# Query weights folded in small array tiles and earlier, output weights split later, key sums copied by ScalarE: a gated mix of linear attention and a dense layer

## The chip, the core and the metric

The kernel runs on one core of a Trainium2 chip. The core's engines run side by side and wait for one another by semaphores: TensorE (PE in the profile; its weight loads are PEld), VectorE (DVE), ScalarE (ACT), GpSimd (POOL) and SyncE (SP), which here only issues DMAs. Matmuls write to PSUM, eight banks of 128 partitions by 512 numbers; everything else lies in SBUF. The metric is the time of one execution on the device, in microseconds (us), as a median over several runs. The profile shows one execution, taken by the hardware profiler.

## What is computed

Two branches over the same 2048 rows of 512 numbers, mixed by a gate of each row, all in float32:

```python
g = _sigmoid((x * gate_w).sum(-1, keepdims=True))
qkv = (x @ wqkv).reshape(B, S, 3, H, Dh)            # H = 32 heads, Dh = 16
pq = jnp.einsum("bhsd,hdf->bhsf", q, w_phi)         # the same for pk from k
phi_q = jnp.concatenate([_softmax(pq), _softmax(-pq)], axis=-1)
kv = jnp.einsum("bhsf,bhsd->bhfd", phi_k, v)
z  = jnp.einsum("bhsf->bhf", phi_k)
o = jnp.einsum("bhqf,bhfd->bhqd", phi_q, kv) / (jnp.einsum("bhqf,bhf->bhq", phi_q, z)[..., None] + 1e-6)
a = o.reshape(B, S, D) @ wo
h = x @ w1 + b1                                     # F = 1792
b = jnp.square(jnp.maximum(h, 0)) @ w2 + b2
return g * a + (1 - g) * b
```

The query projection is followed by a small matrix for each head, so the two can be multiplied once, ahead of all rows: wq times w_phi. The kernel calls this the fold.

## The kernel before

Every large product is made of three matmuls, because each operand is held as a high and a low part (`mm3`, L74 to L78; `split`, L61, makes the two parts: a copy that rounds, then a subtraction). A full matmul has a 128 by 128 stationary operand and 512 columns.

The dense layer gives the order of everything. `work_list` (L843) goes twice over the four blocks of 512 rows, with seven of the fourteen hidden tiles each time. Item t of it makes one hidden tile (`up`, 12 matmuls into a bank named u), two items ahead of its use, and then adds an earlier one to the four output banks (`down`, 12 matmuls into d). All other work is hung between these by hand: `at(step, f, ...)` (L785) files a function under a half step, and the main loop (L870) runs steps 2t, 2t + 0.5, 2t + 1 and 2t + 1.5 ahead of the up product, in its middle, behind it, and in the middle of the down product. So item 25 covers steps 50 to 51.5. Each engine runs its own queue in the order that a scheduler made from this program order and from when it expected things to be ready. `tc.high_priority(offset=AHEAD)` puts an instruction 150 places ahead in that order; `tc.issue_after(i)` keeps an instruction behind i on i's engine.

In the first half of the run (items 0 to 27) the keys are projected, turned into features and multiplied with the values; the key weights were folded at step 5.5 by `tiles_fold` (L175), which works in 32 by 32 tiles of the array, one bank for each of the four row strips. The last key-value product (`kv`, L710) stands at step 53.5. In the second half (items 28 to 55) a pair of row tiles of queries starts every 6 steps from 56.5 on: projection (`do_q`), features (`do_phi`, whose transposed pieces go to phiT by twelve DMAs on SP and four ScalarE copies), the numerator (`do_n`, L380) and the output product with wo (`finish`).

What the change touches:

- `do_wT` (L456) at step 49 loads the query weights and w_phi into five buffers of the tag row, of which there are six. Two tiles of gate rows and the room for the key sums (`kv_room`, step 51) use the same tag.
- `do_fold` (L459) at steps 53, 54, 55 and 56 makes one quarter of the folded query weights each: four full-array float32 matmuls of 128 columns into a bank (`fold`, L148), then the split by ScalarE and VectorE straight from the bank. [...]
- `bank` (L53) hands out the small PSUM banks in turn. At steps 51 to 55 there are three of them: a, e and f. Bank b holds the key sums until `kv_done`.
- `wo_load` and `wo_split` (L235, L241): the output weights, in four tiles, at steps 50.5 to 53.5 and 52 to 55. They use the tag in of the pool `stage`, with four buffers, like the dense weights (`ffn_load`, the last at step 56) and the x tiles (`do_x`, step 61 for the next block). `behind()` (L69) keeps a split behind the newest hidden tile's on ScalarE and VectorE.
- `kv_done` (L747) at step 55 copies the key sums out of their bank by four VectorE copies of 17 partitions and sends the row of sums to DRAM and back to all partitions (z), where the query features need it.
- `gated` (L443) takes the four output banks, times the gate, out at the end of each block.

Of the kernel before, what the change touches and what calls it, by code (L numbers as in the profile page):

```python
# [7 lines left out]
F32 = mybir.dt.float32  # L8
F32R = mybir.dt.float32r
# [6 lines left out]
P = 128  # L16
S, D, H, DH, F = 2048, 512, 32, 16, 1792
NK = D // P
# [16 lines left out]
def tile_gated_mix(ctx: ExitStack, tc: tile.TileContext, xT, xn, wqT, wkT, wphi, wv, wo, w1, b1, w2, b2, gw, out):  # L35
# [112 lines left out]
    def fold(loaded, nm, k):  # L148
        wph, *t = loaded
        ps = bank(f"fold{nm}{k}")  # L150
        for g in range(NK):
            nc.tensor.matmul(ps[:, g * P:(g + 1) * P], t[g][:, k * P:(k + 1) * P], wph[:, g * P:(g + 1) * P],
                             start=True, stop=True)
        hi = wpool.tile([P, 512], F32R, tag=f"wah{k}", name=f"w{nm}h{k}")
        lo = wpool.tile([P, 512], F32R, tag=f"wal{k}", name=f"w{nm}l{k}")
        with tc.high_priority(offset=AHEAD):
            split(ps, hi, lo, nc.scalar, nc.vector)
        return hi, lo

# [14 lines left out]

    def tiles_fold(loaded):  # L175
        wph, *t = loaded
        pss = [bank(f"fold{r}") for r in range(4)]

        def mm(g, r, c):
            rows, cols = slice(32 * r, 32 * r + 32), slice(32 * c, 32 * c + 32)  # L180
            return nc.tensor.matmul(pss[r][cols, g * P:(g + 1) * P],
                                    wph[rows, g * P + 32 * r:g * P + 32 * r + 32],
                                    t[g][rows, :].rearrange("p (k c q) -> p k c q", c=4, q=32)[:, :, c, :],
                                    start=True, stop=True, skip_group_check=True)

        last = None
        for x in [(g, r, c) for g in range(NK) for c in range(4) for r in range(4)]:
            with tc.issue_after(last.ins) if last else nullcontext():
                last = mm(*x)
        for half in range(2):  # L190
            tb = work.tile([P, 2, 4, NK, 32], F32, tag="tb", name="turned", bufs=2)
            for r in range(2):
                with tc.high_priority(offset=AHEAD):
                    st["turned"] = nc.vector.transpose(tb[:, r].rearrange("p g k q -> p (g k q)"), pss[2 * half + r])
            for k in range(NK):
                dst = st["raw"][k].rearrange("p (h z g r f) -> p h z g r f", h=2, z=2, g=2, r=4)
                for h in range(2):
                    nc.scalar.activation(dst[:, h, 0, :, 2 * half:2 * half + 2],
                                         tb[:, :, 2 * h:2 * h + 2, k].rearrange("p r g q -> p g r q"), AF.Copy)

# [258 lines left out]
    def do_fold(nm, k):  # L459
        with tc.issue_after(st["up"].ins):  # L460
            st["wa", nm, k] = fold(st["wT"], nm, k)
        if k == NK - 1:
            st["wa"] = [st["wa", nm, i] for i in range(NK)]
            if nm == "k":
                banks.pop()

# [190 lines left out]
    def pair_steps(p, s):  # L657
# [52 lines left out]
        def kv():  # L710
# [3 lines left out]
            with tc.issue_after(later.ins):  # L714
                kv_chunk(False, p == LASTP, st["kv"], v["phi", n], v["v", n])
# [31 lines left out]
    def kv_done():  # L747
        kvps, kvs = st["kv"], st["kvs"]
        for j in range(4):
            s = slice(32 * j, 32 * j + VW)  # L750
            nc.vector.tensor_copy(kvs[s, :], kvps[s, :])
# [60 lines left out]
    at(49, do_wT, wqT)  # L812
    for k in range(NK):
        at(53 + k, do_fold, "q", k)
    for k in range(NK):
        at(base + 8.5 + k, wo_load, k)
        at(base + 10 + k, wo_split, k)
# [52 lines left out]
    for t, (sw, b, i) in enumerate(work_list):  # L870
# [17 lines left out]
        for c in range(NC):  # L888
# [12 lines left out]
            for j, s in enumerate(halves if end else (ALL,)):  # L901
                gated(ends[j] if end else dps[c], n, o, s)
# [49 lines left out]
```

## Time and profile before

| what | value |
|---|---|
| median of 3 runs | 507.05 us (506.77 to 507.06) |
| the profiled execution | 507.18 us, span 505.4 us |
| granted TensorE clock in it | 0.999 |
| PE busy | 500.7 us of the span |
| VectorE busy | 407.0 us |
| ScalarE busy | 256.6 us |

The profile's page has busy times by engine, a strip of the span in 40 slices, the DMA queues, the chain of work that ended last, and the groups of instructions that cost most. The trace behind it can be asked for instructions in order of time (start, duration, engine, line, operation, output<-input, shape, count), for groups by line and shape (busy time, mean ns of one, idle time before them), for waits, and for DMAs with their time to landing. In a row like `u<-xh,w1h` u is what is written and the rest what is read. Matmuls are pipelined, so a matmul's duration is longer than the distance to the next start, and the distances are what counts on PE.

### The profile page before, as it was taken

How to read it: one execution, taken by the hardware profiler on the slowest of the kernel's cores; microseconds unless marked ns; L12 is line 12 of the kernel's file. 1: busy time of each engine (PE TensorE's matmuls, PEld its weight loads, DVE VectorE, ACT ScalarE, POOL GpSimd, SP SyncE). 2: the span in 40 equal slices, each digit the busy share in tenths (PEclk: the TensorE clock that was granted, in tenths of full speed). 3: DMA queues.
4: the chain of work that ended last, by engine and by line, in shares of the span. 5: the costliest groups of instructions: out<-in, count | busy, mean ns of one | idle time of the engine just before them, and what ended most of it. 6: DMA issues, size and time to landing. Idle time of an engine off the chain costs nothing.

```text
span 505.4 us, 9354 instructions
## 1 busy us (share of the span) xinstructions
PE 500.7 (99%) x3520; PEld 406.1 (80%) x3520; DVE 407.0 (81%) x680; ACT 256.6 (51%) x458; POOL 87.3 (17%) x102
## 2 busy tenths in 40 slices
PE   9999999999999999999999999999999999999997
PEld 5878888788888888888888878788787878788776
DVE  5569957988695979796998989897979796897724
ACT  4887655565253474454674744454455353333540
POOL 1000151204410035000013040212222221112200
PEclk9999999999999999999999999999999999999999
DMA  8858587756854578771265311325112231041112
GB/s 261 291 196 273 198 305 225 237 190 234 285 184 165 183 223 294 265 228 65 83 211 209 98 49 48 99 64 150 49 31 90 71 86 43 8 131 57 38 27 83
DMA packets 45829, 76.13 MB, mean 151 GB/s; under 512 B 6868, under 2 KB 23000, under 8 KB 45784
## 3 DMA queue, kind: packets, MB, share of 16 engines
q1 hardware_dynamic: 36072, 41.78, 26.6%
q10 hardware_dynamic: 6768, 23.79, 13.7%
q0 software_dynamic: 2944, 9.96, 5.5%
q8 instruction: 28, 0.46, 0.4%
q14 instruction: 17, 0.14, 0.1%
HBM read 57.68 MB, written 11.54 MB: 137 GB/s over the span
## 4 chain that ended last, share of the span: by engine, by line
PE 98%; DMA 1%; DVE 0%; issue 0%
PE d L76 10%; PE d L77 10%; PE d L78 10%; PE u L76 10%; PE u L77 9%; PE u L78 9%; PE pX L653 3%; PE q L77 3%; PE att L77 3%; PE att L78 3%; PE att L76 3%; PE q L78 3%; PE q L76 3%; PE pX L655 3%; PE pX L654 3%; PE pY L655 2%
## 5 line engine op out<-in xcount | busy, mean ns | idle before, releaser
L421 ACT ACTIVATE r<-u,b1c 128x512 f32<-128x512 f32 x56 | 38.5, 687 | 122.9 <-PE u L78 121.2
L76 PE MATMUL d<-w2h,hh 128*128 128x512 f32 x222 | 86.9, 391 | 0.0
L77 PE MATMUL d<-w2l,hh 128*128 128x512 f32 x222 | 86.4, 389 | 0.0
L78 PE MATMUL d<-w2h,hl 128*128 128x512 f32 x222 | 86.4, 389 | 0.0
L76 PE MATMUL u<-xh,w1h 128*128 128x512 f32 x212 | 83.6, 394 | 0.0
L77 PE MATMUL u<-xl,w1h 128*128 128x512 f32 x212 | 82.6, 390 | 0.0
L78 PE MATMUL u<-xh,w1l 128*128 128x512 f32 x212 | 82.5, 389 | 0.0
L333 POOL TENSOR_TENSOR ez<-e,z 128x512 f32<-128x512 f32 x32 | 42.9, 1360 | 165.0 <-ACT e L309 165.0
L66 DVE TENSOR_TENSOR hl<-r,hh 128x512 fp32r<-128x512 f32 x56 | 37.8, 676 | 24.3 <-ACT hh L63 24.1
L76 PEld LDWEIGHTS d<-w2h,hh 128*128 128x128 f32 x222 | 41.7, 188 | 9.2 <-issue 0.6
L76 PEld LDWEIGHTS u<-xh,w1h 128*128 128x128 f32 x212 | 39.8, 188 | 11.1 <-issue 2.9
L78 PEld LDWEIGHTS d<-w2h,hl 128*128 128x128 f32 x222 | 41.7, 188 | 8.7
L77 PEld LDWEIGHTS d<-w2l,hh 128*128 128x128 f32 x222 | 41.7, 188 | 8.5
L78 PEld LDWEIGHTS u<-xh,w1l 128*128 128x128 f32 x212 | 39.8, 188 | 8.6 <-DVE w1l L66 0.2
L77 PEld LDWEIGHTS u<-xl,w1h 128*128 128x128 f32 x212 | 39.8, 188 | 7.9
L309 ACT ACTIVATE e<-e 128x1024 f32<-128x1024 f32 x27 | 28.6, 1059 | 26.5 <-DVE e L307 26.1
L291 DVE TENSOR_REDUCE sm<-e 128x64 f32<-128x1024 f32 x27 | 32.8, 1215 | 10.8 <-ACT e L309 10.8
L63 ACT ACTIVATE hh<-r 128x512 fp32r<-128x512 f32 x56 | 35.2, 628 | 1.1
L423 ACT ACTIVATE r<-r 128x512 f32<-128x512 f32 x56 | 34.9, 624 | 0.7
L692 ACT ACTIVATE tmp<-pX 128x512 f32<-128x512 f32 x24 | 14.4, 598 | 30.6 <-PE pX L655 27.0
L374 ACT ACTIVATE phiT<-tb 32x256 f32<-32x256 f32 x64 | 26.4, 412 | 5.8 <-DVE tb L359 4.9
L343 DVE TENSOR_REDUCE dz<-ez 128x64 f32<-128x1024 f32 x16 | 19.4, 1212 | 11.7 <-POOL ez L333 11.7
(182 smaller groups left out, 984.2 us busy)
## 6 DMA issues: line engine op xcount, KB each, us to landing
sloto<-wkeep ACTq DMA_DIRECT2D x30, 512.0 KB, 4.6
in<-in_xT SPq DMA_DIRECT2D x42, 256.0 KB, 4.4
slotez<-wkeep ACTq DMA_DIRECT2D x15, 512.0 KB, 5.0
phiT<-tb SPq DMA_DIRECT2D x192, 32.0 KB, 1.8
in<-in_w SPq DMA_DIRECT2D x23, 256.0 KB, 3.3
part<-row POOLq DMA_DIRECT2D x16, 256.0 KB, 5.5
row<-part SPq DMA_DIRECT2D x16, 256.0 KB, 3.0
out<-row SPq DMA_DIRECT2D x15, 256.0 KB, 2.2
```

The lines of the kernel that those rows point to most:

```text
L63: i = nc.scalar.activation(hi, src, AF.Copy)
L66: st["lo"] = elo.tensor_tensor(lo, src, hi.bitcast(F32), ALU.subtract)
L76: nc.tensor.matmul(o, ah[:, sa], bh[:, sb], start=first, stop=False)
L77: nc.tensor.matmul(o, ah[:, sa], bl[:, sb], start=False, stop=False)
L78: return nc.tensor.matmul(o, al[:, sa], bh[:, sb], start=False, stop=last)
L291: nc.vector.tensor_reduce(sm, e3, AX.X, ALU.add)
L309: nc.scalar.activation(ef, ef, AF.Exp)
L333: nc.gpsimd.tensor_tensor(ez[:, hs, :], e3[:, hs, :], zbc[half], ALU.mult)
L374: nc.scalar.activation(dst, src, AF.Copy)
L421: st["relu"] = nc.scalar.activation(r, ps, AF.Relu, bias=b1c[:, fc:fc + 1])
L423: nc.scalar.activation(r, r, AF.Square)
L655: nc.tensor.matmul(ps, l, wh, start=False, stop=j == 1, skip_group_check=True)
```

## The change

The four full-array folds go. In their place `query_fold` makes the folded query weights in two halves, at steps 51.5 and 54: 32 matmuls each of a 32 by 32 stationary tile and 128 columns, over two row strips of the array into two banks; two VectorE transposes of 32 by 32 squares out of these banks (`turned`, at high priority); and four splits of 256 columns from the turned tile. `tiles_fold` for the keys is written with the same helpers and does what it did. The output weights are loaded at steps 58 to 61 and split at 59.5 to 62.5. The key sums leave their bank by ScalarE copies at high priority. `kv` now notes its last matmul, so that the second half fold stands behind it on PE, and the gated sums of the last block of the first pass are kept behind the newest hidden tile's subtraction on VectorE.

```diff
--- before.py
+++ after.py
@@ -145,18 +145,6 @@
             nc.sync.dma_start(t[g + 1], wT[:, g, :])
         return t
 
-    def fold(loaded, nm, k):
-        wph, *t = loaded
-        ps = bank(f"fold{nm}{k}")
-        for g in range(NK):
-            nc.tensor.matmul(ps[:, g * P:(g + 1) * P], t[g][:, k * P:(k + 1) * P], wph[:, g * P:(g + 1) * P],
-                             start=True, stop=True)
-        hi = wpool.tile([P, 512], F32R, tag=f"wah{k}", name=f"w{nm}h{k}")
-        lo = wpool.tile([P, 512], F32R, tag=f"wal{k}", name=f"w{nm}l{k}")
-        with tc.high_priority(offset=AHEAD):
-            split(ps, hi, lo, nc.scalar, nc.vector)
-        return hi, lo
-
     def both(t):
         return t[:, :512], t[:, 512:]
 
@@ -172,31 +160,47 @@
             st["raw"][k] = r
             st["wv"] = nc.sync.dma_start(two(r)[:, :, 256:], two(wv[k * P:(k + 1) * P, :]))
 
+    def fold_block(loaded, out, g, r, c):
+        wph, *t = loaded
+        rows, cols = slice(32 * r, 32 * r + 32), slice(32 * c, 32 * c + 32)
+        return nc.tensor.matmul(out[cols, g * P:(g + 1) * P], wph[rows, g * P + 32 * r:g * P + 32 * r + 32],
+                                t[g][rows, :].rearrange("p (k c q) -> p k c q", c=4, q=32)[:, :, c, :],
+                                start=True, stop=True, skip_group_check=True)
+
+    def turned(pss, half):
+        tb = work.tile([P, 2, 4, NK, 32], F32, tag="tb", name="turned", bufs=2)
+        for r in range(2):
+            with tc.high_priority(offset=AHEAD):
+                st["turned"] = nc.vector.transpose(tb[:, r].rearrange("p g k q -> p (g k q)"), pss[2 * half + r])
+        return tb
+
     def tiles_fold(loaded):
-        wph, *t = loaded
-        pss = [bank(f"fold{r}") for r in range(4)]
-
-        def mm(g, r, c):
-            rows, cols = slice(32 * r, 32 * r + 32), slice(32 * c, 32 * c + 32)
-            return nc.tensor.matmul(pss[r][cols, g * P:(g + 1) * P],
-                                    wph[rows, g * P + 32 * r:g * P + 32 * r + 32],
-                                    t[g][rows, :].rearrange("p (k c q) -> p k c q", c=4, q=32)[:, :, c, :],
-                                    start=True, stop=True, skip_group_check=True)
-
+        pss = {r: bank(f"fold{r}") for r in range(4)}
         last = None
-        for x in [(g, r, c) for g in range(NK) for c in range(4) for r in range(4)]:
+        for g, c, r in [(g, c, r) for g in range(NK) for c in range(4) for r in range(4)]:
             with tc.issue_after(last.ins) if last else nullcontext():
-                last = mm(*x)
+                last = fold_block(loaded, pss[r], g, r, c)
         for half in range(2):
-            tb = work.tile([P, 2, 4, NK, 32], F32, tag="tb", name="turned", bufs=2)
-            for r in range(2):
-                with tc.high_priority(offset=AHEAD):
-                    st["turned"] = nc.vector.transpose(tb[:, r].rearrange("p g k q -> p (g k q)"), pss[2 * half + r])
+            tb = turned(pss, half)
             for k in range(NK):
                 dst = st["raw"][k].rearrange("p (h z g r f) -> p h z g r f", h=2, z=2, g=2, r=4)
                 for h in range(2):
                     nc.scalar.activation(dst[:, h, 0, :, 2 * half:2 * half + 2],
                                          tb[:, :, 2 * h:2 * h + 2, k].rearrange("p r g q -> p g r q"), AF.Copy)
+
+    def query_fold(half):
+        pss = {r: bank(f"fold{r}") for r in (2 * half, 2 * half + 1)}
+        for g, c, r in [(g, c, r) for g in range(NK) for c in range(4) for r in pss]:
+            with tc.issue_after(st["up"].ins):
+                st["up"] = fold_block(st["wT"], pss[r], g, r, c)
+        tb = turned(pss, half)
+        part_ = lambda t: t.rearrange("p (g r f) -> p g r f", g=NK, f=32)[:, :, 2 * half:2 * half + 2, :]
+        for k in range(NK):
+            if not half:
+                st.setdefault("wa", []).append(tuple(
+                    wpool.tile([P, 512], F32R, tag=f"wa{hl}{k}", name=f"wq{hl}{k}") for hl in "hl"))
+            hi, lo = st["wa"][k]
+            split(tb[:, :, :, k].rearrange("p r g q -> p g r q"), part_(hi), part_(lo), nc.scalar, nc.vector)
 
     def operand(i, j, src, slot=None, ehi=None, elo=None):
         if i in HELD:
@@ -455,14 +459,6 @@
 
     def do_wT(wT):
         st["wT"] = load_fold(wT)
-
-    def do_fold(nm, k):
-        with tc.issue_after(st["up"].ins):
-            st["wa", nm, k] = fold(st["wT"], nm, k)
-        if k == NK - 1:
-            st["wa"] = [st["wa", nm, i] for i in range(NK)]
-            if nm == "k":
-                banks.pop()
 
     def do_joint(j, piece):
         if (j, piece) == (0, 0):
@@ -712,7 +708,7 @@
                 st["kv"] = ps_b.tile([P, 2 * P], F32, tag="s", name="kvps")
             later = kv_chunk(p == 0, False, st["kv"], v["phi", m], v["v", m])
             with tc.issue_after(later.ins):
-                kv_chunk(False, p == LASTP, st["kv"], v["phi", n], v["v", n])
+                st["up"] = kv_chunk(False, p == LASTP, st["kv"], v["phi", n], v["v", n])
 
         at(s - 2 - (p > 0), sums_load, p)
         if p == 0:
@@ -748,7 +744,8 @@
         kvps, kvs = st["kv"], st["kvs"]
         for j in range(4):
             s = slice(32 * j, 32 * j + VW)
-            nc.vector.tensor_copy(kvs[s, :], kvps[s, :])
+            with tc.high_priority(offset=AHEAD):
+                nc.scalar.activation(kvs[s, :], kvps[s, :], AF.Copy)
         nc.sync.dma_start(zrow.rearrange("(j x) -> j x", j=4), kvs[DH::32, :])
         for half in range(2):
             z = hold.tile([P, H * VW], F32, tag="vz", name=f"z{half}")[:, :D]
@@ -810,11 +807,11 @@
         pair_steps(p, 14 + 4.5 * p)
     base = (NB - 1) * SL
     at(49, do_wT, wqT)
+    at(51.5, query_fold, 0)
+    at(54, query_fold, 1)
     for k in range(NK):
-        at(53 + k, do_fold, "q", k)
-    for k in range(NK):
-        at(base + 8.5 + k, wo_load, k)
-        at(base + 10 + k, wo_split, k)
+        at(base + 16 + k, wo_load, k)
+        at(base + 17.5 + k, wo_split, k)
     for i in range(NFH):
         for nm, slot in (("w1", base + 2 * i - 1), ("w2", base + 2 * i + 2)):
             at(slot, ffn_load, nm, NFH + i)
@@ -899,7 +896,8 @@
             dst = part[n] if sw == 0 else out[n * P:(n + 1) * P, :]
             end = t == last and c == NC - 1
             for j, s in enumerate(halves if end else (ALL,)):
-                gated(ends[j] if end else dps[c], n, o, s)
+                with tc.issue_after(st["dve"].ins) if (sw, b) == (0, NB - 1) else nullcontext():
+                    gated(ends[j] if end else dps[c], n, o, s)
                 if sw == 0 or done:
                     st["stored"] = (nc.gpsimd if sw == 0 else nc.scalar if j else nc.sync).dma_start(dst[:, s], o[:, s])
```

## The prediction

> **What bounds the kernel now.** I read the page first: busy times, then the chain that ended last.
>
> ```profile
> span 505.4 us, 9354 instructions
> PE 500.7 (99%) x3520; PEld 406.1 (80%) x3520; DVE 407.0 (81%) x680; ACT 256.6 (51%) x458; POOL 87.3 (17%) x102
> PE 98%; DMA 1%; DVE 0%; issue 0%
> ```
>
> A busy PE alone proves little, because matmul ends are modelled; the chain of waits is the stronger evidence: 98% of it is PE, one matmul after another. So I asked for PE's waits, all of them, and for PE's rows in a quiet stretch.
>
> ```profile
> PE pX L653 <- DMA sloto<-wkeep: 0.2, 1, 0.2
> ...
> 236.55 0.39 PE L76 MATMUL u<-xh,w1h 128*128 128x512 f32 x1
> 239.27 0.39 PE L76 MATMUL d<-w2h,hh 128*128 128x512 f32 x1
> ```
>
> Once it has its first operand, PE waits a single time in the run, for 0.2 us, and not near the change. Between the two rows lie twelve full matmuls: 2.72 us, so 0.227 us from one start to the next. The reader is to see a kernel that is the sum of what PE streams. The change can gain only what PE no longer streams, and loses whatever PE newly waits for. Less work for ScalarE or VectorE is worth nothing in itself. The calibrated span is 505.4 us, that execution took 507.18 us and the median of the runs is 507.05; the costs below are that execution's, and I subtract them from the median, 0.13 us lower.
>
> **The change part by part. The folds on PE.** The chain lists each old query fold, four in all; here are the first and the last.
>
> ```profile
> 244.87 0.89 PE foldq L152 x8
> 257.19 0.89 PE foldq L152 x8
> ...
> 244.48 0.39 PE L78 MATMUL u<-xh,w1l 128*128 128x512 f32 x1
> 245.83 0.40 PE L77 MATMUL d<-w2l,hh 128*128 128x512 f32 x1
> ```
>
> PE's own rows agree (the last two): the full matmul before a fold starts at 244.48, the second one after it at 245.83, which is 1.35 less two pitches, 0.90 us. Four folds are 4 x 0.89 = 3.56 us, and all of it goes.
>
> What comes instead is known from this kernel twice over. The key weights are already folded with 32 by 32 tiles, all four row strips at once (L181), and the attention numerator (L385) runs on eight array tiles, as many as a half of the new fold uses (two row strips by four column strips).
>
> ```profile
> 26.15 0.39 PE L78 MATMUL d<-w2h,hl 128*128 128x512 f32 x1
> 26.46 1.90 PE L181 MATMUL fold<-row 32*32 32x128 f32 x128
> 28.30 0.50 PE L76 MATMUL d<-w2h,hh 128*128 128x512 f32 x1
> 28.63 0.40 PE L77 MATMUL d<-w2l,hh 128*128 128x512 f32 x1
> ...
> 297.15 0.39 PE L78 MATMUL u<-xh,w1l 128*128 128x512 f32 x1
> 297.47 1.09 PE L385 MATMUL num<-phiT,kvb 64*32 64x256 f32 x32
> 298.83 0.40 PE L77 MATMUL u<-xl,w1h 128*128 128x512 f32 x1
> ```
>
> The key fold holds PE from 26.15 to 28.63, 2.48 less two pitches: 2.03 us, of which 1.84 is the fold and 0.19 the two switches of shape (0.31 and 0.33 where 0.23 is the pitch). Half of it, with 64 of the 128 records, would be 0.92 + 0.19 = 1.11 if the overlap stays as it is: that is the lower bound. The numerator streams 32 records of 256 columns on eight tiles, as many columns as 64 records of 128: 1.68 less 0.45, or 1.23 us with its switches. The upper bound is that half as many tiles give half the overlap, so that a half takes as long as the whole, 2.03. I take the numerator's 1.23, because it has the same eight tiles; two halves are 2.46. **PE's own sum: 3.56 - 2.46 = 1.10 us gained**, with ends 3.56 - 2.22 = 1.34 and 3.56 - 4.06 = -0.50.
>
> [...]
>
> **The loads.** The first half runs at step 51.5, where PE now stands at 240.63; the old first fold came at 244.87. The last of its five loads waits for a row buffer.
>
> ```profile
> 236.05 0.35 SPq L145 DMA_DIRECT2D row<-in_wqT  x1
> DMA to landing us min/median/max: 3.1/3.1/3.1
> 240.63 0.39 PE L76 MATMUL d<-w2h,hh 128*128 128x512 f32 x1
> ```
>
> It lands at 239.15, 1.5 us early, and only the last quarter of the half reads it: no wait, though the cover shrinks by four us.
>
> **ScalarE and VectorE.** The groups by shape give the prices.
>
> ```profile
> L66 DVE TENSOR_TENSOR wql<-foldq,wqh 128x512 fp32r<-128x512 f32 x4 | 2.7, 687 | 0.1
> L66 DVE TENSOR_TENSOR wol<-in,woh 128x512 fp32r<-128x512 f32 x4 | 2.7, 679 | 0.0
> L194 DVE STREAM_TRANSPOSE turned<-fold 128x512 f32<-128x512 f32 x4 | 2.5, 685 | 0.4 <-PE fold L181 0.4
> L674 DVE TENSOR_TENSOR vext<-tmp,pY 128x256 f32<-128x256 f32 x24 | 9.9, 414 | 0.1
> L751 DVE COPY row<-kvps 17x256 f32<-17x256 f32 x4 | 1.7, 419 | 0.1
> L672 ACT ACTIVATE e<-pX 128x256 f32<-128x256 f32 x5 | 1.9, 385 | 7.2 <-PE pX L655 7.0
> ```
>
> VectorE gets four transposes (4 x 0.685) and eight half subtractions (no row has the shape and operands; nearest is L674's 0.414; I take it, the bounds 0.34 and 0.69 are a half and a whole of the old one): 6.05 us. It loses four subtractions of 0.687, the four copies of 0.419 and, up to the first query tile, the four output-weight subtractions of 0.679: 7.14. Net 1.1 us less before the first query tile; the 2.7 us of output weights return some 20 us later. ScalarE gets eight halves and four key-sum copies of about 0.385 (4.6 us) for four whole ones; at 51% busy it covers this. The key sums go out to 17 partitions from a bank that no matmul waits for; a copy that is some tenths slower on ScalarE costs nothing.
>
> One place is close: the transposes go ahead of the feature scaling that the last key-value product reads.
>
> ```profile
> 244.99 1.21 DVE L314 TENSOR_TENSOR e<-e,r 128x1024 f32<-128x1024 f32 x1
> 247.06 0.70 PE L323 MATMUL kvps<-e,vext 128*17 128x32 f32 x62
> ```
>
> The scaling ends at 246.20, 0.86 ahead of PE. PE will come 1.23 - 0.89 = 0.34 later; two transposes take 1.37. 1.37 - 0.34 - 0.86 is 0.17 us of wait, if no gap on VectorE takes them up. Two half subtractions in place of whole ones ahead of the scaling give back 2 x 0.27. I cost it at nothing; the bound is 0.2. The wait added for the last block's gated sums puts them behind the newest hidden tile's subtraction; PE writes their banks again 24 matmuls (5.4 us) later, and four instructions, even at the 1.24 us of the widest one quoted here, are done by then: nothing.
>
> **The output weights, and who queues behind them.** This is the part I trust least. Their sixteen loads on SP move to just ahead of the x tiles' (step 61); SP issues nothing from 270.69 to 278.47 (rows below) and has room for them. Both kinds use the same four stage buffers; the new splits stand at 59.5 to 62.5, behind the hidden tile that was made just before. Today the x tiles of the next block (step 61) are all loaded by 270.31 and copied from 281.40 on (the first two rows). Now all four buffers hold output weights until VectorE has subtracted them, which puts those loads where today the loads of the block after stand (the rows behind):
>
> ```profile
> 270.31 0.38 SPq L86 DMA_DIRECT2D in<-in_xT  x1
> 281.40 2.20 ACT L63 ACTIVATE xh<-in 128x512 fp32r<-128x512 f32 x4
> ...
> 279.87 0.68 DVE L66 TENSOR_TENSOR hl<-r,hh 128x512 fp32r<-128x512 f32 x1
> 285.15 1.24 DVE L359 STREAM_TRANSPOSE tb<-e 128x1024 f32<-128x1024 f32 x1
> 287.48 0.67 DVE L66 TENSOR_TENSOR xl<-in,xh 128x512 fp32r<-128x512 f32 x1
> ...
> 278.47 7.61 SPq L368 DMA_DIRECT2D phiT<-tb  x12
> 286.17 1.48 SPq L86 DMA_DIRECT2D in<-in_xT  x3
> 287.75 7.89 SPq L368 DMA_DIRECT2D phiT<-tb  x12
> 295.74 0.53 SPq L86 DMA_DIRECT2D in<-in_xT  x1
> ...
> DMA to landing us min/median/max: 3.2/3.2/3.2
> 299.53 0.39 PE L77 MATMUL u<-xl,w1h 128*128 128x512 f32 x1
> ```
>
> The hidden tile is subtracted at 279.87; of four subtractions behind it three fit ahead of the transpose at 285.15 and the fourth comes after it, at 287.48. So three loads go ahead of the second set of phiT transfers on SP, and the fourth after all twelve, at 295.74. In the new order that fourth load is an x tile that PE needs for its last quarter of the product at 299.53. With everything 1.1 us earlier (VectorE's 1.1, and PE's): issued 294.6, landed 297.8 (3.2), copied 0.55 (2.20 / 4) and subtracted 0.67: 299.0, against 298.4 on PE: **a wait of about 0.6**. I take 0.5, since VectorE may gain a little more than its 1.1 where it stood waiting for the first query tile; the bounds are 0 and 1.0. The twelve phiT transfers themselves (issued by 295.64, read at 297.47) and PE come forward by the same 1.1 us, so that margin stays.
>
> **The sum:** 507.05 - 1.10 + 0.5 = 506.45; I say 506.4.
>
> **The rivals.**
>
> No wait: if the fourth output-weight tile is subtracted before the transpose, or the scheduler places its x load ahead of the second set, all four x tiles are there before PE. For it: the gaps on VectorE ahead of 285.15 are decided by readiness, and readiness shifts. Time 507.05 - 1.10 = 505.95, faster by just over the 0.2% bound (1.01 us), which is about what a measurement of this kernel can tell from no change.
>
> Slower: the same fourth x tile, but its subtraction also queues. VectorE starts a multiplication of features just then, a slow one.
>
> ```profile
> 299.00 2.37 DVE L314 TENSOR_TENSOR e<-e,w 128x1024 f32<-128x1024 f32 x1
> ```
>
> If the x subtraction stands behind it, it ends at 301.37 - 1.1 + 0.67 = 300.9, and PE waits 2.5 us: 507.05 - 1.10 + 2.5 = 508.45. It decides for slower from a wait of 2.1 us on, that is when the fourth x tile is ready later than 300.5. Against it: x tiles come earlier in the program than that multiplication.
>
> The fold does not pay: eight tiles overlap half as well, 2.03 a half, no x wait: 507.05 + 0.50 = 507.55. The numerator's rows speak against it.
>
> [...]
>
> **How the numbers follow.** Forecast (fold gains, short wait) 0.40; no wait 0.32; slower 0.18; fold does not pay 0.10. Faster by over 0.2% takes most of the no-wait case: 0.30. Within 0.2%: the forecast, the rest of no wait and the unpaid fold, 0.50. Slower 0.20, the rival and 0.02 for what no case names. Low end: the fold's lower bound without wait, 507.05 - 1.34 = 505.7. High end 508.0, which leaves out most of the slower case and little else. The forecast's own range is 505.9 to 507.0 (waits of 0 to 1.0).
>
> **What would show it.** L152 gone, two visits of 64 tiled records, 1.2 us each from the full matmul before to the second after: right; 2 us each: the third rival. PE's waits: a row for xl or xh near 298 is the forecast's; none there, the first rival; over 2 us, the second. In SP's rows, the place of the fourth in_xT load against the second phiT set decides between them. A PE wait near 247 on VectorE would show the transposes too costly, and one near 241 on a load would show that the moved fold came too early; both are costed at nothing and would prove me wrong.

## The result, and the profile after

The changed kernel takes 511.84 us (median of 5 runs, 511.48 to 512.05); the kernel before, on the same chip, 507.06 (506.77 to 507.4). The ratio is 1.0088, with a 95% interval of 1.0076 to 1.0099 (the two medians alone give 1.0094): slower by 0.9%, or 4.5 to 4.8 us. I had said 506.4, in a range from 505.7 to 508.0. The profiled execution took 511.76 us.

The changed kernel's page, busy times and the chain that ended last, and then all of TensorE's waits of over 1 us behind its first operand (line, who released it, us in total, times, longest):

```profile
span 510.0 us, 9560 instructions
PE 501.8 (98%) x3616; PEld 404.3 (79%) x3616; DVE 408.2 (80%) x684; ACT 259.0 (51%) x466; POOL 85.8 (17%) x102
PE 87%; DVE 6%; DMA 3%; POOL 1%; SPq 1%; issue 1%; ACT 0%; POOLq 0%
```

```profile
PE att L78 <- DVE o L66: 1.9, 1, 1.9
PE d L78 <- DVE hl L66: 1.4, 1, 1.4
```

The chain was 98% PE and is 87%. PE now waits twice for VectorE, and for neither thing that I had named: not for an x tile, but for the low part of a hidden tile (hl, item 33) and for that of the first numerator (o). PE's rows in order of time (start, duration, engine, line, operation, output<-input, shape, count, idle time before) give the two waits, and the two halves of the fold (64 records each, two for each of a half's 32 matmuls):

```profile
241.19 0.39 PE L78 MATMUL d<-w2h,hl 128*128 128x512 f32 x1
241.51 1.15 PE L166 MATMUL fold<-row 32*32 32x128 f32 x64
242.59 0.50 PE L76 MATMUL d<-w2h,hh 128*128 128x512 f32 x1
242.93 0.40 PE L77 MATMUL d<-w2l,hh 128*128 128x512 f32 x1
...
250.74 0.40 PE L78 MATMUL d<-w2h,hl 128*128 128x512 f32 x1
251.07 1.53 PE L166 MATMUL fold<-row 32*32 32x128 f32 x64
252.53 0.50 PE L76 MATMUL u<-xh,w1h 128*128 128x512 f32 x1
252.86 0.39 PE L77 MATMUL u<-xl,w1h 128*128 128x512 f32 x1
...
300.67 0.39 PE L77 MATMUL d<-w2l,hh 128*128 128x512 f32 x1
302.42 0.50 PE L78 MATMUL d<-w2h,hl 128*128 128x512 f32 x1 [1.36 <-DVE hl L66]
...
306.40 0.39 PE L77 MATMUL att<-wol,o 128*128 128x512 f32 x1
308.72 0.50 PE L78 MATMUL att<-woh,o 128*128 128x512 f32 x1 [1.93 <-DVE o L66]
```

From one start to the next less the pitch of 0.227, the first wait costs 1.52 us and the second 2.09; both matmuls behind them start 0.34 later instead of 0.23, another 0.2. The halves cost 1.74 - 0.45 = 1.29 us and 2.12 - 0.45 = 1.67, so the fold gains 3.56 - 2.96 = 0.60, not 1.10. The first numerator is 0.3 later than its pitch, and the run up to the seventh key product, where both programs are alike, took 0.8 us longer in this execution: 3.8 - 0.6 + 0.3 + 0.8 = 4.3 of the 4.58 us between the two profiled executions.

Who made hl and o late? In the trace of before they are subtracted at these times, with two small steps of the denominators between them:

```profile
289.27 0.68 DVE L66 TENSOR_TENSOR hl<-r,hh 128x512 fp32r<-128x512 f32 x1
297.99 0.24 DVE L349 TENSOR_SCALAR den<-den,gate 128x32 f32<-128x32 f32 x1
298.75 0.22 DVE L351 TENSOR_TENSOR w<-r,den 128x64 f32<-128x64 f32 x1
302.57 1.25 DVE L66 TENSOR_TENSOR o<-num,o 128x512 fp32r<-128x512 f32 x2
```

After the change, SyncE's DMAs, ScalarE, VectorE and GpSimd in order of time (one fence for each):

```profile
279.14 7.59 SPq L372 DMA_DIRECT2D phiT<-tb  x12
286.83 1.96 SPq L86 DMA_DIRECT2D in<-in_xT  x4
288.88 7.47 SPq L372 DMA_DIRECT2D phiT<-tb  x12
```

```profile
285.50 0.69 ACT L425 ACTIVATE r<-u,b1c 128x512 f32<-128x512 f32 x1 [2.27 <-PE u L78]
290.16 0.63 ACT L63 ACTIVATE xh<-in 128x512 fp32r<-128x512 f32 x1 [3.97 <-DMA in<-in_xT]
...
291.80 0.62 ACT L427 ACTIVATE r<-r 128x512 f32<-128x512 f32 x1
...
294.79 0.61 ACT L63 ACTIVATE hh<-r 128x512 fp32r<-128x512 f32 x1
```

```profile
290.83 0.69 DVE L66 TENSOR_TENSOR xl<-in,xh 128x512 fp32r<-128x512 f32 x1 [1.21 <-ACT xh L63]
...
294.92 1.22 DVE L295 TENSOR_REDUCE sm<-e 128x64 f32<-128x1024 f32 x1 [0.26 <-ACT e L313]
297.62 1.22 DVE L347 TENSOR_REDUCE dz<-ez 128x64 f32<-128x1024 f32 x1 [1.48 <-POOL ez L337]
...
301.68 0.68 DVE L66 TENSOR_TENSOR hl<-r,hh 128x512 fp32r<-128x512 f32 x1
...
303.37 0.89 DVE L353 TENSOR_SCALAR den<-den,gate 128x32 f32<-128x32 f32 x1
304.29 1.25 DVE L355 TENSOR_TENSOR w<-r,den 128x64 f32<-128x64 f32 x1
...
308.01 1.25 DVE L66 TENSOR_TENSOR o<-num,o 128x512 fp32r<-128x512 f32 x2
```

```profile
302.92 2.54 POOL L337 TENSOR_TENSOR ez<-e,z 128x512 f32<-128x512 f32 x2 [5.34 <-ACT e L313]
```

Read them from the top. All four x loads go out at 286.83, when the output weights have given up the stage buffers (the last subtraction ends at 284.96) and SyncE is through with the first set of phiT transfers, which now stands ahead of them; before, the last x load went at 270.31. ScalarE stands 3.97 us at the first x copy, and the square of item 33's hidden tile, whose relu ended at 286.19, is queued behind that copy and starts at 291.80. VectorE idles at the x subtractions in turn, 1.21 us at the first and 2.5 in all up to 294.92. ScalarE's part of item 33 (hh) is done at 295.40, but in VectorE's queue hl now stands behind the steps of the query features, 1.48 us of them idle for a GpSimd product, and starts only at 301.68. So hl comes 12.4 us later than before and o 5.4 later; the small steps of the denominators now fall into GpSimd's two products (302.92 to 305.46) and take 2.14 us where they took 0.46. PE never waits for the x tiles themselves.

### The profile page after: what moved, and what is told of

It reads as the page before. It is cut to its first block, busy times and chain, and to the rows that moved or that the text cites. A ratio compares the mean times of both kernels' runs of the same rounds, so it can differ in the third digit from the quotient of the medians.

```text
span 510.0 us, 9560 instructions
## 1 busy us (share of the span) xinstructions
PE 501.8 (98%) x3616; PEld 404.3 (79%) x3616; DVE 408.2 (80%) x684; ACT 259.0 (51%) x466; POOL 85.8 (17%) x102
## 4 chain that ended last, share of the span: by engine, by line
PE 87%; DVE 6%; DMA 3%; POOL 1%; SPq 1%; issue 1%; ACT 0%; POOLq 0%
PE d L76 9%; PE d L77 9%; PE d L78 9%; PE u L76 8%; PE u L77 8%; PE u L78 8%; PE pX L649 3%; PE att L78 3%; PE pX L651 3%; PE att L76 3%; PE att L77 3%; PE pX L650 3%; PE q L77 2%; PE q L76 2%; PE q L78 2%; PE pY L651 2%
```

## The experiments

Theory A: the output weights hold the four stage buffers; the x loads come late, and what is queued behind the x copies on ScalarE and VectorE comes late with them. Theory B: it is VectorE's order alone, four subtractions of 0.68 us more ahead of late operands. Each run is compared with the kernel before on its own chip.

**e1_wo_back: the whole change, but the output weights at their old steps.**

```diff
-        at(base + 16 + k, wo_load, k)
-        at(base + 17.5 + k, wo_split, k)
+        at(base + 8.5 + k, wo_load, k)
+        at(base + 10 + k, wo_split, k)
```

> The changed kernel with the output weights loaded and split at the old steps again (50.5 and 52 on); the folds in halves, the transposes and the ScalarE copies of the key sums stay. Theory (late output weights hold the four stage buffers, the x tiles come 20 us late, and ScalarE and VectorE stand in their queues behind them): the x loads are back by 271 us, the two PE waits near 300 us (1.5 and 2.1 us) are gone, and what is left is what the folds give, 3.58 - 2.94 = 0.6 us: 506.2 to 506.8, ratio 0.999. Rival (the new fold with its transposes and half splits, or the ScalarE copies, put VectorE behind): the waits stay, 510 to 512.

**e2_wo_only: the kernel before with this one step** (the same lines the other way round).

> The kernel of before with one thing changed: output weights loaded at 58 to 61 and split at 59.5 to 62.5. Theory: the same two waits near 300 us without any new fold, 3.5 to 5 us in all: 510.5 to 512. Rival (fold, transposes or ScalarE copies are the cause): within 1 us of 507.1.

Moved back: 507.28 us, ratio 0.9995 [0.9987, 1.0004]. The move alone: 512.82, 1.0107 [1.0089, 1.0124], with the same two waits, 1.9 and 1.3 us. The first is a little above what was expected (506.2 to 506.8), and so is the second (510.5 to 512), which also has a first numerator 1.0 us slower than before. So the moved weights carry the whole loss. But without them the fold gains nothing that shows. One wait of the run with the weights back is new, at the first numerator:

```profile
296.65 0.62 PE L389 MATMUL num<-phiT,kvb 64*32 64x256 f32 x2
297.45 1.09 PE L389 MATMUL num<-phiT,kvb 64*32 64x256 f32 x30 [0.18 <-DMA phiT<-tb]
298.47 0.50 PE L76 MATMUL u<-xh,w1h 128*128 128x512 f32 x1
298.81 0.39 PE L77 MATMUL u<-xl,w1h 128*128 128x512 f32 x1
```

From 296.65 to 298.47 it took 1.82 us, where the kernel before takes 1.03 (297.47 to 298.50): 0.8 us, the fold's gain and more. PE is early, and the features' second set of transfers isn't: it is issued from 288.54 on, where the kernel before has 287.75.

**e3_wo_mid: the weights halfway, so that the x loads are free again.**

```diff
-        at(base + 16 + k, wo_load, k)
-        at(base + 17.5 + k, wo_split, k)
+        at(base + 12 + k, wo_load, k)
+        at(base + 13.5 + k, wo_split, k)
```

> The changed kernel with the output weights 3.5 half steps later than before instead of 7.5: loads at 54 to 57, splits at 55.5 to 58.5. Both free their buffers before the x loads at 61. Theory: it is not lateness as such but the x tiles behind the output weights, so no wait near 300 us: 506.2 to 506.8. Rival (any move of the output weights' VectorE work towards the query features costs in proportion): about half of the loss, 508.5 to 509.5.

**e5_item33_first: nothing moved, but item 33's square and split at high priority** (`first` is `tc.high_priority(offset=AHEAD)`).

```diff
-        with tc.issue_after(after.ins) if after else nullcontext():
+        with tc.issue_after(after.ins) if after else first() if st.get("item") == 33 else nullcontext():
             nc.scalar.activation(r, r, AF.Square)
...
-        st["act"] = split(r, hh, hl, nc.scalar, nc.vector)
+        with first() if st.get("item") == 33 else nullcontext():
+            st["act"], st["dve"] = split(r, hh, hl, nc.scalar, nc.vector), st["lo"]
```

> The changed kernel with the square and the split of one hidden tile (item 33) at high priority, so that ScalarE and VectorE do them between the x tiles' splits and not behind them; nothing else in any queue moves. If the two PE waits are two independent losses: the 1.5 us wait for that tile goes and the other stays, 510.3. If VectorE's queue is late as a whole and the second wait is set by it: the first wait goes, the second grows by as much, 511.5 to 512. I lean to the second.

Halfway, 510.7 us, 1.006 [1.0046, 1.0075]: not what A alone expects, and more than its rival's 508.5 to 509.5. The two late operands are gone, and in their place PE waits at the first numerator:

```profile
PE num L389 <- DMA phiT<-tb: 1.8, 1, 1.8
```

From PE's rows this stop costs more than the wait itself: 4.86 us from the full matmul before the numerator to the second one behind it, where the kernel before takes 1.68. The subtractions now stand among the first query tile's features on VectorE (261.4 to 273.1 us); that they make the features late was not tested by itself. With item 33 first, 512.49 us, 1.01 [1.0081, 1.0119]: the wait for hl is gone and the one for o has grown from 1.9 to 3.5 us; behind that longer stop TensorE's next seven matmuls took 3.09 us from start to start instead of 1.59. Taking one operand out of a late queue helps nothing while the next one is as late.

**e3_wo_late: the weights later still.**

```diff
-        at(base + 16 + k, wo_load, k)
-        at(base + 17.5 + k, wo_split, k)
+        at(base + 21 + k / 2, wo_load, k)
+        at(base + 23.5 + k / 2, wo_split, k)
```

> The changed kernel with the output weights later still: loads at 5 half steps after the change's own (two to a step), splits 6 to 4.5 half steps later. Mine, that the loss comes from the four stage buffers which the weights hold while the next block's four x loads and ScalarE's queue wait for them: here the x loads take the buffers first, the square and splitting of the item behind are on time, and TensorE's waits for the hidden tile and for the second attended operand go, or the latter shrinks under 1 us: 506.6 to 508.5 us. Rival, that the subtractions of the output weights lie ahead of the numerator's own low part on VectorE wherever they stand after the query features began: the wait for o stays at 1.5 us or more, 509.5 us or more. Second rival: the output weights come after the first use of them, a wait of TensorE for the weights themselves.

514.39 us, 1.0129 [1.0114, 1.0144]. The x loads come first here, hl is on time (290.39) and its wait is gone, as A has it. The second rival took the time: the weights' loads stand behind the transposed features on SyncE, and PE needs them first.

```profile
PE att L76 <- ACT woh L63: 4.4, 1, 4.4
```

**e9_own_buffers: the changed kernel, its steps untouched, the raw output weights in the two tiles that later hold the numerators.** That takes the held buffers away and leaves the subtractions on VectorE.

```diff
-        t = st["wo", k] = stage.tile([P, 512], F32, tag="in", name="in")
+        if k % 2 == 0: st["wo2"] = both(work.tile([P, 2 * D], F32R, tag=f"o{k // 2}", name="wo2", bufs=1))
+        t = st["wo", k] = st["wo2"][k % 2].bitcast(F32)
```

> The changed kernel, its output weights at its own half steps, but loaded into the two tiles that later hold the numerators (free between the last key pair and the first numerator) and not into the four stage buffers, so the next block's x loads need not wait for them; the four subtractions of the weights stay on VectorE among the query features. Theory of the held buffers: the x loads are issued before the first set of transposed features (SyncE, about 257 to 272 us), ScalarE's wait of 4 us for them and VectorE's 2.5 us of idle time behind it go, and with these both waits of TensorE near 300 us shrink from 1.4 and 1.9 us to under 0.5 us each: 506.8 to 508.5 us. Rival, that the order of VectorE's queue alone does it (the subtractions ahead of the hidden tile's and the numerator's low parts, 2.6 us in all): the waits stay within 0.7 us of what they were, 510.5 us or more.

508.09 us, 1.0013 [1.0004, 1.0022]: of 0.88% only 0.13% is left. ScalarE's row has all four x copies without a gap (the first fence); VectorE's and GpSimd's rows (the next two) show what is left:

```profile
281.44 2.20 ACT L63 ACTIVATE xh<-in 128x512 fp32r<-128x512 f32 x4
```

```profile
298.03 0.68 DVE L66 TENSOR_TENSOR hl<-r,hh 128x512 fp32r<-128x512 f32 x1
...
299.71 0.90 DVE L353 TENSOR_SCALAR den<-den,gate 128x32 f32<-128x32 f32 x1
300.64 1.25 DVE L355 TENSOR_TENSOR w<-r,den 128x64 f32<-128x64 f32 x1
...
304.36 1.25 DVE L66 TENSOR_TENSOR o<-num,o 128x512 fp32r<-128x512 f32 x2
```

```profile
299.27 2.54 POOL L337 TENSOR_TENSOR ez<-e,z 128x512 f32<-128x512 f32 x2 [5.34 <-ACT e L313]
```

PE's waits there:

```profile
PE att L78 <- DVE o L66: 0.5, 1, 0.5
```

The held buffers made most of it; B, as the cause alone, is out. Both operands come 3.65 us earlier than in the changed kernel (298.03 against 301.68, 304.36 against 308.01), some 3.1 of it net, since this execution was 0.6 ahead at the seventh key product. But hl is still 8.8 us later than in the kernel before, behind steps of the query features as in the changed kernel, and PE does not wait for it: that much slack it had, and only what the held buffers put on top was too much. The 0.5 us left is o's. Its two small steps end about when GpSimd's products do: at 300.61, the first product at 299.27 + 1.27 = 300.54; and at 301.89, the pair at 301.81.

**e13_product_dve: the same, with the fourth query tile's two products on VectorE.**

```diff
-            nc.gpsimd.tensor_tensor(ez[:, hs, :], e3[:, hs, :], zbc[half], ALU.mult)
+            (nc.vector if n == 3 else nc.gpsimd).tensor_tensor(ez[:, hs, :], e3[:, hs, :], zbc[half], ALU.mult)
```

> As the run with buffers of their own, but the two denominator products of the fourth query tile are made by VectorE, between the small operations of the third tile's denominators, instead of by GpSimd beside them. If it is GpSimd's products that stretch VectorE's small multiplications (0.90 and 1.25 us against 0.24 and 0.22 us elsewhere), both return to under 0.3 us here; VectorE has two products of some 0.65 us in their place, so the wait for the numerator's low part stays between 0 and 0.7 us and the time within 0.6 us of the run it is made from. Rival, that something else stretches them (the waits for another engine's result): they stay over 0.8 us.

```profile
300.37 0.23 DVE L353 TENSOR_SCALAR den<-den,gate 128x32 f32<-128x32 f32 x1
...
301.11 0.22 DVE L355 TENSOR_TENSOR w<-r,den 128x64 f32<-128x64 f32 x1
```

Both are back to 0.23 and 0.22 us, o ends earlier, and PE waits for nothing near 300: 507.47 us, 0.9998 [0.9989, 1.0007], with the output weights still at the change's late steps. So GpSimd's products beside them had stretched them: in e9 each small step ends about as one product ends (0.07 and 0.08 us after it). Why they do, no run shows.

**e10_own_late_split and e11_own_pool** (both from e9) try to take the subtractions out of the way as well: later, or on GpSimd.

```diff
-        at(base + 17.5 + k, wo_split, k)
+        at(base + 21.5 + k / 2, wo_split, k)
```

```diff
-            split(st["wo", k], hi, lo, nc.scalar, nc.vector)
+            split(st["wo", k], hi, lo, nc.scalar, nc.gpsimd)
```

> As the run with buffers of their own, with the weights' splits 2.5 to 4 half steps later, so that on VectorE they stand behind the low part of the hidden tile of item 33 and ahead of the numerator's. Theory that each late operand is set by what stands ahead of it on VectorE: the wait for the hidden tile is gone, that for the numerator's low part is between 0 and 1.5 us; 506.6 to 508.5 us. Rival, that the lateness is in the query features themselves (the second pair's transposes): 509 us or more.

> As the run with buffers of their own, with the weights' four subtractions on GpSimd instead of VectorE: neither the held buffers nor the 2.6 us of VectorE are left, the steps stay where the change put them. If these two are the whole cause: no wait of TensorE near 300 us, and the time of the run with the weights moved back, 506.6 to 507.7 us. Rival, that something else of the late step costs (the GpSimd subtractions, some 1.3 us each by its 128x512 products, delay the products of the denominators that stand on the same engine): over 508.5 us.

Later: 508.88 us, 1.0029 [1.0017, 1.004], just above what was expected. The wait for hl is gone, that for o is 1.0 us: ScalarE can't write the numerators' tiles until the raw weights in them are subtracted. On GpSimd: 508.33, 1.0021 [1.0008, 1.0035], between what the two expected; no wait near 300, but a first numerator late by 1.1 us. **e12_own_pool_behind** (e11 with the order of the next run) missed too: 508.66 us, 1.0029 [1.0018, 1.0041], with a numerator late by 1.8, as its rival had it. Why GpSimd's subtractions delay the features was not followed further.

> As the run with the subtractions on GpSimd, with the three input loads between the two sets of transposed features kept behind the second. If both the waits near 300 us and the late first numerator are gone, only the fold's gain is left: TensorE's time from the last key pair to the first numerator is 0.3 to 0.7 us shorter than before and the time 506.3 to 507.1 us. Rival, that GpSimd's subtractions delay the first pair's features: a first numerator late by 0.5 us or more, 507.5 us or more.

**e6_x_behind: the weights back (e1), and the three x loads between the two sets of features kept behind the second.**

```diff
-        with tc.issue_after(st["act"].ins):
+        with tc.issue_after(st["act"].ins), tc.issue_after(st["set2"].ins) if b == NB + 2 else nullcontext():
             st["x", b] = load_x(b % NB)
```

Here `set2` is the last phiT transfer of the second query tile.

> The changed kernel with the output weights back at their old half steps, and the three input loads that SyncE issued between the two sets of transposed query features kept behind the second set (they took 1.48 us of SyncE ahead of it). Mine, that the fold gains 0.64 us and the late first numerator ate it (0.8 us): the second set is issued 1.5 us earlier, the wait of the first numerator for its last feature tile goes, and the time is 506.4 to 506.9 us, 0.2 to 1.1 us under the same kernel with the loads between. Rival, that the query features were late on VectorE and not on SyncE's queue, so the numerator is no earlier: 507.2 us or more. Second rival, that the loads behind the second set come too late for the first block's next projections: a wait of TensorE for an x tile, above 507.5 us.

**e8_before_x_behind: the same order in the kernel before; e7_fold_only: e1 with the key sums copied by VectorE again.**

```diff
-            with tc.high_priority(offset=AHEAD):
-                nc.scalar.activation(kvs[s, :], kvps[s, :], AF.Copy)
+            nc.vector.tensor_copy(kvs[s, :], kvps[s, :])
```

> The kernel before, with nothing but the same three input loads kept behind the second set of transposed query features. Mine: the kernel before has no wait at its first numerator that these loads cause, so its time stays within 0.3 us of the kernel before (506.8 to 507.4 us); then what the run with both edits gains belongs to the fold. Rival, that the order of the loads is a gain by itself: 0.5 us or more under the kernel before, and the fold adds nothing.

> The fold alone: output weights at their old half steps and the key sums copied by VectorE as before. Mine: the copies on ScalarE are worth little; VectorE gets four small copies more (about 0.3 us each) ahead of the first query tile, which makes the first pair's features, and so the first numerator, up to 1 us later than in the run with the weights moved back: 507.3 to 508.3 us. Rival, that the ScalarE copies cost rather than gain (they stand in ScalarE's queue ahead of the first activations): 506.8 us or less.

e6, which expected 506.4 to 506.9: 507.53, 0.9996 [0.9987, 1.0005]; e8: 507.22, 0.9994 [0.9986, 1.0003]; e7: 507.73, 1.0003 [0.9993, 1.0012]. By time all three are the kernel before; e8 and e7 lie where they were expected, but e7's numerator is no later than e1's. By PE's rows e6 did what it should: its numerator takes 1.03 us again. One stretch tells more than the medians here: from the second matmul behind the seventh key product to the second behind the first numerator, which holds the fold and all that hangs on it. Its ends in before, and in e6:

```profile
229.95 0.39 PE L654 MATMUL pX<-sloto,sh 128*128 128x512 f32 x1
...
298.83 0.40 PE L77 MATMUL u<-xl,w1h 128*128 128x512 f32 x1
```

```profile
229.90 0.39 PE L650 MATMUL pX<-sloto,sh 128*128 128x512 f32 x1
...
298.43 0.40 PE L77 MATMUL u<-xl,w1h 128*128 128x512 f32 x1
```

68.88 us before, 69.03 in e1, 68.53 in e6: a gain of 0.35, within the spread of the runs, and a third of the 1.10 forecast. The rest is nearly all a pause in the second half of the fold, 0.62 us here between one small matmul and the next, for which the profile names no semaphore.

**e14_half_earlier: e6 with the second half one step earlier.**

```diff
-    at(54, query_fold, 1)
+    at(53, query_fold, 1)
```

> The run with the weights moved back and the loads kept behind, with the second half of the query fold one step (two matmul groups) earlier. The second half had a pause of 0.36 to 0.6 us in the middle, with no wait that the profile names, and the first half none. If the pause belongs to the place (something else that runs then), it goes or changes here, the second half costs 1.28 us as the first, and TensorE's time from the last key pair to the first numerator is another 0.3 to 0.6 us shorter: 506.2 to 507.2 us. Rival, that it belongs to the second half wherever it stands: the same 1.6 to 2.0 us and the same time as the run it is made from.

506.86 us, 0.9988 [0.998, 0.9997], in the range expected. Both halves now take 1.29 us, but the stretch is no shorter than e6's (68.67 us): the pause hasn't gone; it has moved into the key product that follows. PE's rows, and the DMA queues in the stretch 248 to 250.2 us (queue, kind, packets, MB, share):

```profile
250.09 0.36 PE L327 MATMUL kvps<-tmp,vext 128*17 128x32 f32 x21
251.06 0.54 PE L327 MATMUL kvps<-tmp,vext 128*17 128x32 f32 x41 [0.60 <-issue]
```

```profile
q8 instruction: 1, 0.02, 2.7%
```

So neither of the two expectations was quite right. In all thirteen kernels here with the new fold and the ten warm-up matmuls (the changed one and twelve runs) the pause, 0.24 to 0.80 us, stands right behind the 2250th matmul record (counted from 0), whatever that is. And in all thirteen the 2251st starts 2.3 to 2.7 us after the last transfer of kind "instruction" on queue q8 began, one packet of 16 KiB (the page of the changed kernel has 28 of them, 0.46 MB); in this run it began at 248.65.

**e15_thirty_more: e14 with the ten warm-up matmuls of 512 columns cut into forty of 128; e17_before_thirty: the same in the kernel before.**

```diff
-        idle(10)
+        idle(40)
...
-            st["up"] = nc.tensor.matmul(st["warm"], st["zeros"][:, :P], st["zeros"], start=True, stop=True)
+            st["up"] = nc.tensor.matmul(st["warm"][:, :P], st["zeros"][:, :P], st["zeros"][:, :P], start=True, stop=True)
```

> The run with the second half one step earlier, with the ten 512-column matmuls that TensorE does on zeros before the inputs land cut into forty of 128 columns (the same time of the array, 30 records more ahead of everything). In six kernels the pause stood right after the 2250th matmul record, whatever that record was (in the second half of the fold, or in the key product behind it, 0.24 to 0.80 us). If it belongs to the number of the instruction in TensorE's stream, it now falls among full matmuls, where a stop of the instructions is covered by what is queued: the key product behind the halves takes 1.5 us as in the kernel before, both halves 1.28 us, TensorE's time from the last key pair to the first numerator is 67.9 us against 68.9 us before, and the time is 506.0 to 506.8 us. Rival, that it belongs to the fold or to that moment of the run: a pause of 0.2 us or more again among the small matmuls between 240 and 246 us, and 506.8 us or more.

> The kernel before with the same forty short matmuls at its start, as a control. It has no small matmuls near the 2250th record, so nothing to gain: 506.8 to 507.5 us, within 0.2 us of the kernel before. Rival, that the forty records themselves change the time (an earlier or a later start of the first projections): 0.4 us or more to either side, which would then have to be taken off the other run's result.

```profile
250.52 0.70 PE L327 MATMUL kvps<-e,vext 128*17 128x32 f32 x62
...
251.07 0.74 PE L327 MATMUL kvps<-tmp,vext 128*17 128x32 f32 x62
```

The key product runs through, both halves take 1.29 us, and no pause stands among the small matmuls there. The reason expected is not the right one: the 2250th record does not fall among full matmuls but into the key product's first row above, and the next one starts 4 ns behind it. That full matmuls cover such a stop was the author's estimate, and no run shows a stop covered; in the trace of before no two matmuls start more than 0.34 us apart in the 5 us after any of its 28 packets of that kind began. What differs is the transfer: the last packet of instructions before that record began at 244.47, 6.5 us ahead of the 2251st instead of 2.3 to 2.7.

The stretch is 68.33 us, of which 0.43 is a slower numerator again, put down to the features since PE comes earlier still, though the profile names no wait there; without it 67.90, the 67.9 expected. Time: 506.58 us, 0.998 [0.997, 0.9991], 0.2% faster than the kernel before, and the lowest ratio here. (The profiled execution was the slowest of this kernel's, 508.4 us, but lost its time ahead of the stretch.) The control: 507.43, 0.9995 [0.9984, 1.0006]. The stretch accounts for 0.55 us of the 1.0 us gained; where the rest lies was not looked for.

So the pause goes with the record number and the packet, and not with the fold. In thirteen kernels it stands among dense small matmuls (64 in 1.08 us, 17 ns from one to the next in the changed kernel). That a late packet of instructions makes it is an inference that fits all runs; no run moved the packet alone, and why it came earlier in e15 is not shown.

## Why the prediction was wrong

- **The step that failed is "The output weights, and who queues behind them".** It found the place: the stage buffers, and x loads held until the output weights are subtracted. It then asked only when TensorE needs the x tile. It did not ask what stands behind the x copies on ScalarE and the x subtractions on VectorE while they wait, in queues that are worked in order: item 33's square (started 5.6 us after its relu had ended) and split, the next features, the numerator's low part. The wait forecast was 0.5 us at an x tile; measured were 1.52 and 2.09 at hl and o, and none at the x tile. e2 shows the move to carry the loss, e9 that the held buffers make most of it (0.75 of 0.88%), and e13 that without GpSimd's products beside the small steps no loss is left.
- **Three loads between the feature sets and one behind** was wrong as well: all four subtractions fitted ahead of the second transpose (287.20), and all four loads went together at 286.83. That is the condition of the first rival, no wait, and the wait came all the same, elsewhere.
- **The slower rival had the right sign and the wrong mechanism**: no x subtraction queued behind the multiplication L314.
- **The fold on TensorE**: the numerator as a model was good, 1.29 us for a half against 1.23. The sum of 1.10 measured 0.60: 0.12 went to the 0.06 us more of each half, the rest to the pause in the second half, which no row of before could show. With the pause out of the way, in e15, the fold gives 0.98, of which the late numerator takes 0.43.
- **"That margin stays" (the phiT transfers)** failed. In e1 the two transposes came 0.8 us later than before (278.00 and 285.94 against 277.20 and 285.15) although PE came 0.8 earlier, so the first numerator waited and took the fold's gain back. VectorE's 1.1 us ahead of the first query tile is not 1.1 us of the features: their chain runs through ScalarE, GpSimd and SyncE too. Which of these held it is not shown.
- **The rest held**: no wait at the moved fold's loads, none at the key product for the transposes, nothing clear of the noise from the key sums on ScalarE (1.0003 in e7 against 0.9995 in e1), and no wait that points to the gated sums. The small matmuls' 17 ns (64 in 1.08 us) leave no place for the rival in which the fold does not pay on the array.

## What to carry to other kernels

When a load is made to wait for a buffer, price not the tile that comes late but every instruction behind its first reader on each engine that works its queue in order, as ScalarE did here with item 33's square (5.6 us), up to the one TensorE needs next. Work taken off TensorE is a gain only as far as the chain that feeds its next stage has slack; look for that slack before counting it. A dense burst of small matmuls (17 ns from one to the next) paused here for 0.24 to 0.80 us where the profile names no wait; the pauses ended 2.3 to 2.7 us after a packet of instructions began, so the instruction transfers are worth a look before the burst itself is blamed.

## What was not expected of the hardware

- After the longer waits TensorE ran slower for a while: in e3_wo_late, behind a stop of 4.8 us, eight matmuls started 0.38 to 0.43 us apart instead of 0.227, at a granted clock of 0.52 (315.6 to 319.0 us). In e5, behind 3.9 us, the next seven took 3.09 us instead of 1.59, and the mean granted clock of that execution was 0.995; in e3_wo_mid, behind 2.4, the clock was 0.57 from 299 to 303 us. Behind the 1.5 and 2.1 us of the changed kernel the pitch was 0.23 from the second matmul on, at a granted clock of 1.000.
- Beside a GpSimd product of 1.27 us a VectorE step of 64 columns took 1.25 us, in the changed kernel and in e9; without one beside it, in before and in e13, it took 0.22.
- The pause of 0.24 to 0.80 us at one record number in TensorE's stream, ended 2.3 to 2.7 us after a 16 KiB packet of instructions began, in thirteen kernels; with the packet 6.5 us ahead, in e15, there was none.
